# Block 0's loads in two queues, masks apart, first weights asked for ahead of the values

## The chip, the core and the metric

The kernel runs on one core of a Trainium2 chip. A core has TensorE (PE in the profile) for matrix products, VectorE (DVE), ScalarE (ACT) and GpSimd (POOL) for the rest, and SyncE (SP), which here does nothing but issue DMAs. Every engine works through its own instructions in order and waits on semaphores. SP and ACT can each issue DMAs into a hardware queue of their own; the packets of both queues run on the same 16 DMA engines. The metric is the device time of one execution in microseconds; runs are compared by their medians.

## What is computed

Three steps, one behind the other, all in fp32: attention over 4 x 8 heads of 576 positions with 64 columns, a gated feed-forward layer behind an RMS norm, and a second gated layer.

```python
mask_local = (rel >= 0) & (rel < 32)                        # heads 0..3
mask_strided = (rel >= 0) & (pos_k % 32 == pos_q % 32)      # heads 4..7
attn = softmax(where(mask, q @ k.T / 8, -1e9)) @ v
x = attn.transpose(0, 2, 1, 3).reshape(2304, 512)
x = x / sqrt(mean(x * x) + 1e-6) * rms_g
x = (silu(x @ w_gate) * (x @ w_val)) @ w_out                # 512 -> 1536 -> 512
out = (x @ w_a) * (x @ w_b) @ w_out2                        # 512 -> 1536 -> 512
```

## The kernel before

**Blocks.** The 2304 tokens are cut into six blocks t of 384 (96 positions of each of 4 batches). A block runs through attention, then through twelve chunks fc of 128 hidden columns: `mm_in` makes the gate sums `g_ps` and the value sums `v_ps` (12 matmuls each), VectorE and ScalarE make `h` of them, `split` cuts `h` into a high and a low part `hl`, and `emit_y` adds the chunk's share to `y` with 12 more matmuls. Attention of block t+1 is woven into the chunks of block t. A last stage does the second layer for all blocks.

**Products in three passes.** `mm3` makes every fp32 product of three matmuls, high by high, high by low and low by high. So weights and activations are held in two parts each. The weights arrive raw and are converted once, while block 0 runs: `words` takes two ScalarE steps (L137, L142), one VectorE step (L145), then `parts` casts on ScalarE (L150) and subtracts on GpSimd (L151). For chunk 0 the gate and the value weights are converted in two halves of 512 columns; from chunk 1 on both go through in one step of 1024. The tile `cz` between them has two buffers for gate and value weights, so that a third L142 waits for the first L151.

**Attention of block 0** is not woven into anything: until it is done, TensorE has no chunk to work on. The local heads run on TensorE in three groups g: scores (`qk`, L296), mask and scale (`smask`, L314), row maximum (`lmax`, L323), exponentials (`lexp`, L336 and L333), division (`lnorm`, L346 to L348), transposition (`pt`, L358, with the identity matrix, and `ptc`, L368), product with the values (`pv`, L378). The strided heads need no matrix product: `sqk` multiplies on GpSimd (L248) and sums on VectorE (L251), then `ssub`, `sexp` (L264), `snorm` (L270 to L273), and `spv` multiplies by the values on GpSimd (L281) and sums on VectorE (L284). The product tile has two buffers, so the third product waits for the first sum. The results `xx` (L387 high, L389 low) are the right-hand sides of chunk 0, and `rinv` (L448, L450) is the norm that all gates of the block need.

**What sets the order.** The list `LOADS0` says in which order the loads of block 0 are written, `STEPS0` the order of its steps; behind them a scheduler orders each engine's instructions by a timeline of its own. So a moved load also moves compute instructions. Before, SP issues all loads, and the constants `cst_sb` (identity, both masks and the norm's gains, 194 KB) come in one DMA behind the strided queries `qs_t` and keys `kv_t`, whose rows are 768 bytes long. There are eight completion semaphores for the DMAs; a ninth waits until the first has landed. The raw weights follow behind all of block 0's loads: `load_units(NFC)` asks for twelve units of two 512 KB tiles, gate and value weights of chunk 0 first.

## Time and profile before

| | |
|---|---|
| median of three runs | 964.13 us (962.64 to 965.04) |
| profiled execution, its own time | 965.19 us |
| its span in the trace | 963.4 us |
| busy share of the span: PE, DVE, ACT, POOL | 97 %, 65 %, 44 %, 56 % |
| mean granted clock of TensorE | 0.986 |

The profile is of one execution, 1.8 us of which lie outside the span, and this execution took 1.06 us more than the median. Times in the trace count from the start of the span. In a timeline a row is: start, duration, engine, line, operation, what is written and read, shape, count, and in brackets how long the engine sat idle before it and what ended that wait. SPq stands for the DMAs that SP issues; their duration is that of the issue. In a table of windows each engine has its busy time and its number of instructions, then come TensorE's granted clock, the share of time in which the DMA engines were busy, and GB/s.

### The profile page before, as it was taken

To read this page: it belongs to the slowest core of one execution; us is meant where nothing else is said; L and a number is where in the kernel's file an instruction comes from. 1 tells how busy PE (TensorE), PEld (TensorE's weight loads), DVE (VectorE), ACT (ScalarE), POOL (GpSimd) and SP (SyncE) were. 2 spreads that over 40 slices of the span, in tenths; PEclk is the share of its full clock that TensorE was granted. 3 is DMA by queue.
4 is the path that set the end of the run, shared out by engine and by line. 5 is a ranking of instruction groups with operands and counts; after the bars stand their busy time and mean duration, and the time that the engine had idled before them with its cause. 6 is when DMAs were issued, how large, how long until landed. Compare 5 with 4: busy or idle time off the path is not lost.

```text
span 963.4 us, 14134 instructions
## 1 busy us (share of the span) xinstructions
PE 936.9 (97%) x5324; PEld 889.0 (92%) x5324; DVE 624.8 (65%) x913; ACT 421.7 (44%) x792; POOL 541.8 (56%) x407
## 2 busy tenths in 40 slices
PE   5998999999999999999999999999999999999998
PEld 4798999999999999999999898999999999999997
DVE  5669867548818895987566378667655655464534
ACT  5987655334433433444555455435425422122110
POOL 3568946458749687969379545654734424123211
PEclk6899999999999999999999999999999999999999
DMA  9964375426534553532788975997993973753701
GB/s 344 408 258 157 110 281 195 159 99 215 175 105 149 174 179 111 177 129 66 270 332 307 358 267 202 369 422 278 359 383 118 341 295 131 290 235 147 259 31 66
DMA packets 57507, 215.55 MB, mean 224 GB/s; under 512 B 5984, under 2 KB 14816, under 8 KB 51808
## 3 DMA queue, kind: packets, MB, share of 16 engines
q1 hardware_dynamic: 57296, 214.53, 61.0%
q8 instruction: 42, 0.69, 0.3%
q14 instruction: 25, 0.20, 0.1%
q10 hardware_dynamic: 144, 0.13, 0.0%
HBM read 172.17 MB, written 42.47 MB: 223 GB/s over the span
## 4 chain that ended last, share of the span: by engine, by line
PE 65%; DVE 7%; POOL 6%; DMA 5%; ACT 4%; issue 4%; SPq 0%; DVEq 0%; ACTq 0%; POOLq 0%
PE o L925 5%; PE o L923 5%; PE o L924 5%; POOL prod L248 4%; DMA raw<-in_w 4%; PE Y L856 4%; PE Y L855 4%; PE Y L854 4%; PE y L482 3%; PE Z L856 3%; PE Z L855 3%; PE Z L854 3%; PE y L483 3%; PE X L854 3%; PE X L856 2%
## 5 line engine op out<-in xcount | busy, mean ns | idle before, releaser
L151 POOL TENSOR_TENSOR hl<-c,hl 128x384 fp32r<-128x384 f32 x72 | 77.4, 1076 | 180.2 <-ACT hl L150 173.6
L248 POOL TENSOR_TENSOR prod<-kv_t,qs_t 128x512 f32<-128x512 f32 (+12 forms) x57 | 107.3, 1903 | 21.5 <-DMA wo<-wod 9.7
L482 PE MATMUL y<-hl,wo 128*128 128x384 f32 x288 | 98.3, 345 | 4.8 <-DVE hl L507 3.7
L281 POOL TENSOR_TENSOR prod<-kv_t,S_t 128x512 f32<-128x512 f32 (+12 forms) x57 | 86.8, 1536 | 22.5 <-issue 8.2
L481 PE MATMUL v_ps<-xx,gv 128*128 128x384 f32 x288 | 97.2, 337 | 1.9 <-DVE sg L760 1.9
L481 PE MATMUL g_ps<-xx,gv 128*128 128x384 f32 x288 | 97.6, 339 | 0.6 <-DVE sg L764 0.6
L482 PE MATMUL v_ps<-xx,gv 128*128 128x384 f32 x288 | 97.6, 339 | 0.0
L483 PE MATMUL v_ps<-xx,gv 128*128 128x384 f32 x288 | 97.2, 338 | 0.0
L483 PE MATMUL g_ps<-xx,gv 128*128 128x384 f32 x288 | 97.1, 337 | 0.0
L482 PE MATMUL g_ps<-xx,gv 128*128 128x384 f32 x288 | 96.8, 337 | 0.0
L861 DVE TENSOR_TENSOR c<-c,Y 128x384 f32<-128x384 f32 x108 | 58.9, 550 | 58.0 <-PE Y L856 53.6
L483 PE MATMUL y<-hl,wo 128*128 128x384 f32 x288 | 95.4, 340 | 0.0
L507 POOL TENSOR_TENSOR hl<-h,hl 128x384 fp32r<-128x384 f32 x60 | 64.9, 1081 | 51.1 <-ACT hl L506 51.0
L284 DVE TENSOR_REDUCE xs_t<-prod 128x64 f32<-128x448 f32 (+17 forms) x57 | 85.9, 1521 | 10.5 <-POOL prod L281 9.4
L481 PE MATMUL y<-hl,wo 128*128 128x384 f32 x288 | 83.7, 342 | 3.7 <-ACT hl L506 2.1
L924 PE MATMUL o<-slab,hl 128*128 128x512 f32 x214 | 83.7, 392 | 0.0
L923 PE MATMUL o<-slab,hl 128*128 128x512 f32 x214 | 83.7, 392 | 0.0
L925 PE MATMUL o<-slab,hl 128*128 128x512 f32 x214 | 82.5, 394 | 0.0
L150 ACT CAST hl<-c 128x384 fp32r<-128x384 f32 x72 | 37.0, 514 | 94.9 <-DVE c L891 94.6
L856 PE MATMUL Y<-slab,form 128*128 128x384 f32 x216 | 73.1, 338 | 0.0
L855 PE MATMUL Y<-slab,form 128*128 128x384 f32 x216 | 73.0, 338 | 0.0
L854 PE MATMUL Y<-slab,form 128*128 128x384 f32 x216 | 73.0, 338 | 0.0
(148 smaller groups left out, 2463.5 us busy)
## 6 DMA issues: line engine op xcount, KB each, us to landing
form<-formd SPq DMA_DIRECT2D x32, 1792.0 KB, 10.6
wo<-wod SPq DMA_DIRECT2D x60, 512.0 KB, 4.1
raw<-in_w SPq DMA_DIRECT2D x40, 512.0 KB, 7.2
gv_raw<-in_w SPq DMA_DIRECT2D x32, 512.0 KB, 10.1
formd<-form SPq DMA_DIRECT2D x6, 1792.0 KB, 7.5
formd<-forms SPq DMA_DIRECT2D x6, 1792.0 KB, 12.5
slab<-x2d SPq DMA_DIRECT2D x24, 384.0 KB, 4.0
wod<-wo SPq DMA_DIRECT2D x12, 512.0 KB, 3.2
```

The costliest lines, as they stand in the source:

```text
L248: nc.gpsimd.tensor_tensor(pr, st["ks", g][:, :, :n, :], st["qs"][:, heads(g), mm:mm + 1, :].to_broadcast([128, G, n, D]), op=ALU.mult)
L281: st["pvm"] = nc.gpsimd.tensor_tensor(pr, st["vs", g][:, :, :n, :], st["S"][:, heads(g), mm, :n, None].to_broadcast([128, G, n, D]), op=AL ...
L284: st["pvr"] = nc.vector.tensor_reduce(st["xs"][:, mm, heads(g), :], pr.rearrange("p g n d -> p g d n"), axis=X, op=ALU.add)
L481: nc.tensor.matmul(out_ps, w_hi, x_hi, start=start, stop=False)
L482: nc.tensor.matmul(out_ps, w_hi, x_lo, start=False, stop=False)
L483: nc.tensor.matmul(out_ps, w_lo, x_hi, start=False, stop=stop)
L854: nc.tensor.matmul(bank(n), hi, x[p][:, 0, c], start=begins and c == 0, stop=False, skip_group_check=not begins)
L855: nc.tensor.matmul(bank(n), hi, x[p][:, 1, c], start=False, stop=False, skip_group_check=not begins)
L856: nc.tensor.matmul(bank(n), lo, x[p][:, 0, c], start=False, stop=c == 1, skip_group_check=not begins)
L923: nc.tensor.matmul(o, h[:, 0, cols], w[0], start=n == 0, stop=False)
L924: nc.tensor.matmul(o, h[:, 0, cols], w[1], start=False, stop=False)
L925: nc.tensor.matmul(o, h[:, 1, cols], w[0], start=False, stop=n == len(chunks) - 1)
```

## The change

The loads of block 0 are spread over two queues. SP keeps the local queries, the strided queries, the values and the weights; ACT issues the local keys `k_t`, the masks, the strided keys, the last third of the second half's queries, and the identity matrix. The constants are two tensors now: `mask_sb` (both masks and the gains, 130 KB) is asked for behind the first queries and keys, `cst_sb` is the identity matrix alone (64 KB) and comes later. The strided queries of every block, and the strided keys and values of block 0, are laid out on the host so that each partition reads one piece of 3072 bytes instead of four of 768. The first unit of raw weights is asked for ahead of the values. And the load of the square root's table waits for the strided exponential too.

```diff
-LOADS0 = "la0 lq ls0 cst la1 lb0 lvl1 lb1 lvl0 lv0"
+LOADS0 = "la0 masks lq ls0 la1 lb0 lb1 w0 cst lvl1 lv0 lvl0"
...
+        second = nc.scalar if t == 0 else nc.sync
...
-                nc.sync.dma_start(k_t, ktl[t, hf])
+                second.dma_start(k_t, ktl[t, hf])
...
-                nc.sync.dma_start(st["q", hf][:, 512:], qtl[t, hf, :, 512:])
+                (second if hf else nc.sync).dma_start(st["q", hf][:, 512:], qtl[t, hf, :, 512:])
...
-            nc.sync.dma_start(q_t, qs[:, :, 3 * t:3 * t + 3, :])
+            nc.sync.dma_start(q_t, qs[t])
...
-                nc.sync.dma_start(k_t, src[:, heads(g), :L, :])
+                if t == 0:
+                    (second if key == "ks" else nc.sync).dma_start(k_t, {"ks": ks0, "vs": vs0}[key])
+                else:
+                    nc.sync.dma_start(k_t, src[:, heads(g), :L, :])
...
-            with tc.issue_after(st["exp"].ins):
+            with tc.issue_after(st["exp"].ins), tc.issue_after(st["sexp"].ins):
...
-    cst_sb = const1.tile([128, 388], F32, name="cst_sb")
-    ident = cst_sb[:, 0:128]
+    cst_sb = const1.tile([128, 128], F32, name="cst_sb")
+    mask_sb = const1.tile([128, 260], F32, name="mask_sb")
+    ident = cst_sb
...
-    s0["cst"] = lambda: nc.sync.dma_start(cst_sb, cst)
+    s0["masks"] = lambda: nc.scalar.dma_start(mask_sb, masks)
+    s0["cst"] = lambda: nc.scalar.dma_start(cst_sb, cst)
+    s0["w0"] = lambda: load_units(1)
...
-    load_units(NFC)
+    load_units(NFC - 1)
```

No compute instruction is added or taken away; the line numbers of the changed kernel are up to 8 higher. The scheduler moves instructions in block 0 and at the head of block 1 on every engine; behind the first quarter of TensorE's rows the orders are the same again.

**The start, SP and ACT.** Here `q_t` and `k_t` are the local heads' queries and keys, `qs_t` and `kv_t` the strided heads', `v_t` the local values, `gv_raw` the raw weights. SP before:

```order
L207 DMA q_t<-in_qtl 128x512
L208 DMA k_t<-in_ktl 128x512
L227 DMA qs_t<-in_qs 128x4x192
L236 DMA kv_t<-in_ks 128x4x192
L569 DMA cst_sb<-in_cst 128x388
L207 DMA q_t<-in_qtl 128x512
L208 DMA k_t<-in_ktl 128x512
L213 DMA q_t<-in_qtl 128x256
L219 DMA v_t<-in_vl 128x512
L213 DMA q_t<-in_qtl 128x256
L219 DMA v_t<-in_vl 128x512
L236 DMA kv_t<-in_vs 128x4x192
```

SP now:

```order
L208 DMA q_t<-in_qtl 128x512
L228 DMA qs_t<-in_qs 128x768
L208 DMA q_t<-in_qtl 128x512
L214 DMA q_t<-in_qtl 128x256
L111 DMA gv_raw<-in_w 128x1024 x2
L220 DMA v_t<-in_vl 128x512
L238 DMA kv_t<-in_vs 128x768
L220 DMA v_t<-in_vl 128x512
L111 DMA gv_raw<-in_w 128x1024 x22
```

Five loads and the constants left SP, and two tiles of weights stand ahead of the values. ACT now, where the table load and eight exponentials in a row stood first:

```order
L209 DMA k_t<-in_ktl 128x512
L574 DMA mask_sb<-in_masks 128x260
L238 DMA kv_t<-in_ks 128x768
L209 DMA k_t<-in_ktl 128x512
L214 DMA q_t<-in_qtl 128x256
L575 DMA cst_sb<-in_cst 128x128
L340 ACT_TABLE_LOAD
L340 ACTIVATE s_t,lsm<-s_t,lmx 128x96 x4
L137 ACTIVATE gv_raw<-gv_raw 128x512
L142 ACTIVATE cz<-gv_raw 128x512
L340 ACTIVATE s_t,lsm<-s_t,lmx 128x96 x4
```

Six issues stand ahead of the table load, and the first two steps on weights stand between the exponentials of group 0 and those of group 1; before they came behind both. On VectorE, in the same place, the division of group 0 (L348 of the code before) now stands ahead of the maximum of group 1, and the third sum of the values' products stands behind one more weight step than before.

**ACT at chunk 1.** The rows where the weights of chunk 1 (128x1024) and the right-hand sides `xx` are made. Before:

```order
L137 ACTIVATE gv_raw<-gv_raw 128x1024
L142 ACTIVATE cz<-gv_raw 128x1024
L387 ACTIVATE xx<-att,cst_sb 128x384
L432 ACTIVATE sq<-att 128x384
L150 CAST gv<-cz 128x2x512
L387 ACTIVATE xx<-att,cst_sb 128x384
L432 ACTIVATE sq<-att 128x384
L387 ACTIVATE xx<-att,cst_sb 128x384 x2
```

Now:

```order
L137 ACTIVATE gv_raw<-gv_raw 128x1024
L142 ACTIVATE cz<-gv_raw 128x1024
L391 ACTIVATE xx<-att,mask_sb 128x384
L436 ACTIVATE sq<-att 128x384
L391 ACTIVATE xx<-att,mask_sb 128x384
L436 ACTIVATE sq<-att 128x384
L150 CAST gv<-cz 128x2x512
L391 ACTIVATE xx<-att,mask_sb 128x384 x2
```

The second right-hand side and its square moved ahead of the weights' cast.

**DVE late in block 0.** `hl` is the split that TensorE's y matmuls wait for, L776 and L778 the two steps before it, L145 the step on weights; L251, L260 and L346 to L348 belong to block 1's attention. Before:

```order
L778 SCALAR_TENSOR_TENSOR v_ps<-th,v_ps 128x384
L760 SCALAR_TENSOR_TENSOR sg<-g_ps,rinv 128x384
L346 TENSOR_SCALAR lsm<-lsm 64x8
L347 RECIPROCAL lrs<-lsm 64x8
L348 TENSOR_TENSOR s_t<-s_t,lrs 64x512
L251 TENSOR_REDUCE S_t<-prod 128x2x6
L776 TENSOR_TENSOR v_ps<-sg,v_ps 128x384
L145 SCALAR_TENSOR_TENSOR cz<-gv_raw,cz 128x1024
L260 TENSOR_REDUCE smx<-S_t 128x12
L507 TENSOR_TENSOR hl<-v_ps,hl 128x384
```

Now:

```order
L783 TENSOR_TENSOR v_ps<-sg,v_ps 128x384
L255 TENSOR_REDUCE S_t<-prod 128x2x5
L350 TENSOR_SCALAR lsm<-lsm 64x8
L351 RECIPROCAL lrs<-lsm 64x8
L145 SCALAR_TENSOR_TENSOR cz<-gv_raw,cz 128x1024
L352 TENSOR_TENSOR s_t<-s_t,lrs 64x512
L767 SCALAR_TENSOR_TENSOR sg<-g_ps,rinv 128x384
L785 SCALAR_TENSOR_TENSOR v_ps<-th,v_ps 128x384
L145 SCALAR_TENSOR_TENSOR cz<-gv_raw,cz 128x512
L255 TENSOR_REDUCE S_t<-prod 128x2x6
L783 TENSOR_TENSOR v_ps<-sg,v_ps 128x384
L511 TENSOR_TENSOR hl<-v_ps,hl 128x384
```

The wide step on weights stood between L778 and the split; now it stands ahead of the step that answers to L778, and a narrow one is in its place.

## Rows read from the trace of the kernel before

**Rows 1.** Windows of the whole program: busy us (instructions) by engine, PEclk, DMA share, GB/s.

```profile
10.00:34.00 24.00, 17.30 (x115) 13.69 (x115) 15.40 (x33) 19.44 (x44) 11.85 (x8) 0.59 1.03 407
...
42.00:58.00 16.00, 12.83 (x59) 11.70 (x60) 8.61 (x15) 15.97 (x24) 6.69 (x3) 0.89 1.04 406
58.00:88.00 30.00, 30.00 (x191) 29.27 (x189) 25.75 (x40) 24.27 (x60) 26.67 (x15) 1.00 0.46 153
88.00:96.00 8.00, 4.50 (x19) 4.44 (x19) 7.47 (x11) 4.60 (x9) 4.06 (x3) 0.79 0.50 172
96.00:130.00 34.00, 34.00 (x219) 32.58 (x218) 27.12 (x36) 23.30 (x40) 25.74 (x17) 1.00 0.39 140
130.00:960.00 830.00, 824.89 (x4661) 786.34 (x4659) 531.69 (x768) 324.88 (x609) 459.12 (x353) 1.00 0.60 220
```

**Rows 2.** Waits of PE from 34 us on: us in total, times, longest.

```profile
PE y L482 <- DVE hl L507: 3.7, 2, 3.5
```

**Rows 3.** Timeline of the first 25 us, the steps of block 0's attention.

```profile
0.73 1.28 ACT L336 ACT_TABLE_LOAD   x1 [0.73 <-PEq L1034]
...
5.29 1.23 PE L296 MATMUL att<-k_t,q_t 128*128 128x96 f32 x8
...
8.25 0.56 DVE L314 SCALAR_TENSOR_TENSOR s_t<-att,cst_sb 128x384 f32<-128x384 f32 x1 [7.17 <-DMA cst_sb<-in_cst]
...
9.05 0.54 DVE L323 TENSOR_REDUCE lmx<-s_t 128x4 f32<-128x384 f32 x1
...
9.63 0.38 ACT L336 ACTIVATE s_t<-s_t,lmx 128x96 f32<-128x96 f32 x1 [7.62 <-DVE lmx L323]
...
10.34 3.89 PE L296 MATMUL att<-k_t,q_t 128*128 128x96 f32 x24 [3.82 <-DMA k_t<-in_ktl]
...
12.36 0.56 DVE L314 SCALAR_TENSOR_TENSOR s_t<-att,cst_sb 128x384 f32<-128x384 f32 x1 [2.05 <-PE att L296]
...
13.54 0.37 ACT L336 ACTIVATE s_t<-s_t,lmx 128x96 f32<-128x96 f32 x1 [2.37 <-DVE lmx L323]
...
14.99 0.64 ACT L137 ACTIVATE gv_raw<-gv_raw 128x512 f32<-128x512 f32 x1
...
15.54 0.66 ACT L142 ACTIVATE cz<-gv_raw 128x512 uint32<-128x512 uint16 x1
...
24.64 1.15 ACT L137 ACTIVATE gv_raw<-gv_raw 128x1024 f32<-128x1024 f32 x1
```

**Rows 4.** The local keys' tile: issue of its DMAs in ns and us, time to landing.

```profile
L208 SPq DMA_DIRECT2D k_t<-in_ktl x2: 415/424/432, 1.2 to 4.1; - x2
...
DMA to landing us min/median/max: 2.9/4.5/6.1
```

**Rows 5.** The same of the raw gate and value weights up to 30 us.

```profile
L111 SPq DMA_DIRECT2D gv_raw<-in_w x20: 327/328/581, 8.2 to 28.6; - x20
...
DMA to landing us min/median/max: 6.2/10.2/10.8
```

**Rows 6.** Windows of 1 us while the strided queries and keys are loaded.

```profile
3.00:4.00 1.00, 1.00 (x6) 0.70 (x5) 0.00 (x0) 0.00 (x0) 0.00 (x0) 1.00 0.75 228
...
5.00:6.00 1.00, 1.00 (x8) 0.94 (x7) 0.00 (x0) 0.00 (x0) 0.00 (x0) 1.00 1.02 288
```

**Rows 7.** Timeline around chunk 1's first weights, POOL and ACT.

```profile
22.01 2.46 POOL L281 TENSOR_TENSOR prod<-kv_t,S_t 128x768 f32<-128x768 f32 x1 [1.02 <-DVE xs_t L284]
...
25.75 1.14 ACT L142 ACTIVATE cz<-gv_raw 128x1024 uint32<-128x1024 uint16 x1
...
29.29 1.04 ACT L150 CAST gv<-cz 128x1024 fp32r<-128x1024 f32 x1 [1.42 <-DVE cz L145]
...
32.02 1.17 ACT L137 ACTIVATE gv_raw<-gv_raw 128x1024 f32<-128x1024 f32 x1
```

**Rows 8.** Timeline of DVE before PE's long wait in block 0.

```profile
87.83 3.08 DVE L145 SCALAR_TENSOR_TENSOR cz<-gv_raw,cz 128x1024 uint32<-128x1024 uint32 x1
```

**Rows 9.** The window behind that wait.

```profile
91.10:94.40 3.30, 2.83 (x9) 2.84 (x10) 3.30 (x7) 2.21 (x6) 0.64 (x1) 0.50 0.72 218
```

More of the change, by code (lines that the diff above doesn't have):

```diff
@@ L77, in fused_kernel @@
 @with_exitstack
-def fused_kernel(ctx: ExitStack, tc: tile.TileContext, qtl, ktl, vl, qs, ks, vs, cst, w1, w2, out):
+def fused_kernel(ctx: ExitStack, tc: tile.TileContext, qtl, ktl, vl, qs, ks, vs, ks0, vs0, masks, cst, w1, w2, out):
     nc = tc.nc
@@ L515, in fused_kernel @@
     const1 = cpool.enter_context(tc.tile_pool(name="const1", bufs=1))
-    cst_sb = const1.tile([128, 388], F32, name="cst_sb")
-    ident = cst_sb[:, 0:128]
-    mask_a = cst_sb[:, 128:320].rearrange("p (a k) -> p a k", a=2)
-    mask_b = cst_sb[:64, 320:384].rearrange("p (a k) -> p a k", a=1)
-    g_sb = cst_sb[:, 384:388]
+    cst_sb = const1.tile([128, 128], F32, name="cst_sb")
+    mask_sb = const1.tile([128, 260], F32, name="mask_sb")
+    ident = cst_sb
+    mask_a = mask_sb[:, 0:192].rearrange("p (a k) -> p a k", a=2)
+    mask_b = mask_sb[:64, 192:256].rearrange("p (a k) -> p a k", a=1)
+    g_sb = mask_sb[:, 256:260]
     pts = [const1.tile([128, 4, 2, PB], F32, name=f"pt{hf}") for hf in range(2)]
@@ L1003, in st @@
         return a[:, 4:].reshape(B, 4, NM, W, D)
-    r["qs"] = c(st(q).transpose(0, 3, 1, 2, 4).reshape(128, 4, NM, D))
+    r["qs"] = c(st(q).transpose(0, 3, 1, 2, 4).reshape(128, 4, NB, NM // NB, D).transpose(2, 0, 1, 3, 4))
     r["ks"] = c(st(k).transpose(0, 3, 1, 2, 4).reshape(128, 4, NM, D))
     r["vs"] = c(st(v).transpose(0, 3, 1, 2, 4).reshape(128, 4, NM, D))
+    r["ks0"], r["vs0"] = (c(r[n][:, :, :NM // NB]) for n in ("ks", "vs"))
     def ok(rows, n):
@@ L1010, in ok @@
         return (j > i) & (j <= i + W), j
-    cst = np.zeros((128, 388), np.float32)
-    cst[:, 0:128] = np.eye(128)
+    cst = np.zeros((128, 260), np.float32)
     m, j = ok(128, 96)
-    cst[:, 128:224] = np.where(m & (j >= W), BIG, NEG)
-    cst[:, 224:320] = np.where(m, BIG, NEG)
-    cst[:64, 320:384] = np.where(ok(64, 64)[0], BIG, NEG)
-    cst[:, 384:] = np.asarray(inputs["moe_rms_g"]).reshape(NCC, 128).T
-    r["cst"] = cst
+    cst[:, 0:96] = np.where(m & (j >= W), BIG, NEG)
+    cst[:, 96:192] = np.where(m, BIG, NEG)
+    cst[:64, 192:256] = np.where(ok(64, 64)[0], BIG, NEG)
+    cst[:, 256:] = np.asarray(inputs["moe_rms_g"]).reshape(NCC, 128).T
+    r["masks"] = cst
+    r["cst"] = np.eye(128, dtype=np.float32)
     def weights(a, b, o):
```

## The prediction, made before the changed kernel ran

> **What bounds the kernel now.** I read the table of windows first, because shares over the whole span say nothing about a change in the first 30 us. From 130 to 960 us TensorE is busy 824.89 of 830 us, from 58 to 88 and from 96 to 130 us without a gap [rows 1]. So the program is one long TensorE stretch, and a load at the start can only shorten what comes ahead of it. From 10 to 34 us TensorE does little that counts, and the DMA engines are busy throughout (share 1.03, 407 GB/s). From 42 to 58 us the bound is ScalarE, 15.97 of 16 us busy, while TensorE has 12.83 [rows 1]: block 0's weights are converted there. From 88 to 96 us TensorE has 4.50 of 8 us; its wait for VectorE's split of 3.5 us lies there [rows 2]. Behind 58 us the DMA share is 0.52 or less until 130 [rows 1], so loads have slack.
>
> Then the timeline of the start. VectorE's first mask step stands at 8.25 us, 7.17 us idle, ended by the DMA of the constants; the scores it wants were done at 5.29 + 1.23 = 6.52. The second scores start at 10.34 because the second keys land then: issued at 4.1, 6.1 to landing [rows 3, 4]. In both waits ScalarE stands idle, 7.62 and 2.37 us [rows 3]. ScalarE is the engine with the long row of work from there on, so what fills or removes its idle time moves everything behind it.
>
> **Step 1, the masks.** They land early now and the scores decide: mask step at 6.6, its maximum next (the change's order has no sum in between), 0.56 + 0.54, first exponential at 7.7 instead of 9.63: 1.9 us earlier. If the masks came as late as 8.2 this would be nothing. The price is on ScalarE: six issues of about 0.42 us (SP's issue of the same keys [rows 4]), the last two waiting for the keys' and the masks' landing, and then the table load of 1.28 us, which was done by 2.0 [rows 3]. The first two loads of before needed 2.9 us from issue (the shorter of the two landings) [rows 4], so I put keys and masks at 3.7 to 5.0, the table at 6.5: hidden under the wait for the scores and the maximum until 7.7, with 1.2 us to spare. Were that cover gone, each us of delay would cost one.
>
> **Step 2, the second scores.** Up to the second keys 1,986 KB stood in the queue; now 1,922 KB in two queues count (896 on SP, 1,026 on ACT). At the old pace they land at 9.9 instead of 10.2. A faster pace is possible: while the strided rows of 768 bytes pass, the engines are busy (1.02) and move only 288 GB/s, against 407 later, and in 3 to 4 us a quarter of their time is free [rows 6, 1]. 768 KB at 407 instead of 288 save 0.8 us, the free time perhaps 0.5: 8.6 at the earliest. I take 9.2, the middle. The scores need 2.0 us as before (10.34 to 12.36), the mask step is at 11.2, and the second exponential follows after the 1.18 us of before plus the division of group 0, which the new order puts ahead of the maximum (a step like the maximum's, 0.54), less the small step that left (0.1): 12.8 instead of 13.54, 0.7 earlier (0 to 1.4).
>
> Here the Trainium skill speaks against the change, on the page "DMA: Bandwidth & Descriptors": under "Issuing engines are not separate DMA queues" it says that DMAs issued from several engines run on the same 16 DMA engines, so that a second issuer saves the issue time alone, and under "Specifications" that rows of 512 bytes or more run at line rate. By the two this step would be worth 0. The second rule does not fit [rows 6], the first may; it is a rival below.
>
> **Step 3, chunk 0's weights.** A pair of weight steps takes 1.2 us (0.64 and 0.66, overlapping). The first pair moves from behind the second exponentials (14.99) into ScalarE's gap before them, from 9.3 to 12.8; for this its tile must land by 11.6. Before, it landed at 8.2 + 6.2 = 14.4 at the earliest [rows 5]; now 2,754 KB of loads count up to it instead of 3,650, which at the 407 GB/s of the queue is 2.3 us less: 12.1. I expect it between 10.5 (faster pace of step 2) and 12.1; either way it fits in part. Between 14.99 and 24.64, the start of chunk 1's weights [rows 3], ScalarE loses that 1.2 us and a wait of about 0.6 us for the transposed rows. So chunk 1's first step could start at 24.64 - 0.7 - 1.8 = 22.1.
>
> **Step 4, what is late next.** It is GpSimd. Chunk 1's second step (25.75) needs a buffer that GpSimd frees when it has split chunk 0's first half, and that comes behind the third product of the values, at 22.01 after a wait of 1.02 us for VectorE's first sum [rows 7]. In the new order that sum stands behind one more weight step; this step needs ScalarE's third pair, which ends about 3.0 us ahead of chunk 1's start, at 19.1. With 0.7 for the weight step and 0.36 for the sum, the product starts at 20.3, 1.7 earlier. So of the 2.5 us of step 3, 1.7 get through here: chunk 1's second step at 24.05.
>
> **Step 5, a gap that closes.** ScalarE waited 1.42 us ahead of chunk 1's cast (29.29) for VectorE [rows 7]. The new order puts the second right-hand side and its square in that wait, 0.95 us. Chunk 2's weights, at 32.02 before, start at 32.02 - 1.7 - 0.95 = 29.4: 2.6 earlier. The norm, the first gates and TensorE's first chunk hang on the same row and move with it.
>
> **The sum.** 42 to 58 us is ScalarE's stretch without idle time, then come GpSimd, VectorE and TensorE in turn; no row there is tied to a time of the DMA queue. So the 2.6 us pass through: 965.19 - 2.6 = 962.6 for the profiled execution, which took 1.06 more than the median, hence 961.5 against the median of 964.13. Bounds from the steps: 1.6 (step 2 at 0, a third of the gap left) to 3.3 (step 2 at 1.4): 960.8 to 962.5. Other blocks' strided queries in one piece: I count 0, TensorE waits for none of them; at most some 0.1 us each of queue time.
>
> What the sum cannot give is the new order of block 0. Differences of orders have no row, so I bound them by the one wait that is there: 3.5 us [rows 2], behind a weight step of 3.08 us on VectorE [rows 8], and then 3.3 us in which TensorE, after that wait, was granted 0.50, the lower of its two levels, 1.2 GHz [rows 9]; a stretch at half pace gives back 1.65. Together 5.1 us either way.
>
> **Rivals.** (a) *The long wait shrinks.* The split now follows three short steps behind the one it depends on, not the wide weight step. If 1.1 to 3.5 us of it go: 958.0 to 960.4. Against it: the wide step moved ahead of that earlier step, so the chain may be as long. (b) *A new wait eats the gain.* That same place: the step that answers to L778 waits behind a weight step of 1.2 to 3.08 us, TensorE waits for it: 962.7 to 964.6, with half of the following slow stretch up to 966. (c) *The loads do not come earlier*, the first rule above as a mechanism: both queues at the old pace, keys at 9.9, weights at 12.1. Step 2 gives 0, step 3 loses half of its pair, step 4 gives 0.9 and step 5 stays: 1.8 in all, 962.3; if the gap of step 5 does not close, 963.2. (d) *Slower*: a second long wait with a slow stretch behind it, 5.1 us, against a gain at its lower end of 1.6: 967.6. It decides once TensorE, between 58 and 88 us, meets a wait long enough that the granted clock falls; GpSimd and VectorE are busy 26.67 and 25.75 of 30 us there [rows 1], so the room is small.
>
> **How the numbers follow.** The measurement can tell about 0.3 %, 2.9 us: below 961.2 is faster, above 967.0 slower. The sum goes through (960.4 to 962.7): 0.58, of which 0.21 lies below 961.2. (a) 0.22, faster. (b) 0.11, same. (c) 0.03, same. (d) 0.06, slower. So faster 0.43, same 0.51, slower 0.06. The likeliest time is 961.5. The range of 958.0 to 964.8 holds the sum, nearly all of (a), most of (b) and (c), and leaves out (d) and the tails, together about 0.16.
>
> **What would show it.** In the changed kernel's timeline: first mask step at 6.6 behind the scores, not behind a DMA; first exponential at 7.7; second scores at 8.6 to 9.9; a pair of 512-wide weight steps ahead of the second exponentials; third product of the values at 20.3; chunk 2's first weight step at 29.4. If these stand and the time does not follow, look at TensorE's waits and the granted clock between 58 and 130 us. The table load ending behind 7.7, or keys landing behind 10 us, would make steps 1 or 2 wrong.

## The result and the profile after

The changed kernel takes 969.29 us (median of six runs, 968.69 to 970.79), the kernel before on the same chip 962.35 (961.00 to 965.04): a ratio of 1.0071 with a 95 % interval of 1.0054 to 1.0088. It is about 7 us slower, where 961.5 was forecast. The profiled execution took 969.16 us (its span is 967.0). That is 4.0 us over the 965.19 of the profiled execution of before, which took 2.8 more than the median of these runs, so the two traces show a little over half of the difference.

First the table of windows of the changed kernel, in the stretches of [rows 1] (columns as there), with the part behind 130 us in two stretches; then the kernel before in these two:

```profile
10.00:34.00 24.00, 17.39 (x118) 13.77 (x118) 18.20 (x35) 20.36 (x40) 11.83 (x9) 0.62 1.03 409
42.00:58.00 16.00, 12.84 (x70) 12.06 (x71) 9.35 (x16) 15.97 (x25) 6.73 (x3) 1.00 1.04 411
58.00:88.00 30.00, 28.34 (x176) 26.76 (x174) 27.43 (x37) 22.53 (x57) 25.28 (x14) 1.00 0.39 133
88.00:96.00 8.00, 6.54 (x39) 5.97 (x39) 7.55 (x17) 6.62 (x11) 2.15 (x3) 1.00 0.57 200
96.00:130.00 34.00, 31.23 (x198) 29.48 (x197) 24.50 (x28) 19.59 (x35) 25.27 (x17) 1.00 0.26 93
...
130.00:210.00 80.00, 76.13 (x469) 72.54 (x469) 50.51 (x82) 38.13 (x85) 42.55 (x39) 1.00 0.60 202
210.00:960.00 750.00, 746.25 (x4178) 711.45 (x4177) 484.49 (x686) 291.84 (x530) 417.21 (x316) 1.00 0.61 223
```

Before:

```profile
130.00:210.00 80.00, 78.62 (x490) 76.18 (x489) 47.93 (x82) 33.27 (x80) 45.71 (x40) 1.00 0.57 190
210.00:960.00 750.00, 746.28 (x4173) 710.15 (x4171) 483.76 (x687) 291.62 (x529) 413.41 (x314) 1.00 0.61 223
```

Behind 210 us the two kernels are alike (746.25 and 746.28 of 750). The loss lies ahead of it: from 58 to 88 and from 96 to 130 us TensorE was busy without a gap [rows 1], and now lacks 1.7 and 2.8 us; from 130 to 210 it lacks 3.9 where it lacked 1.4. The granted clock is 1.00 in all these stretches: the half pace of [rows 9] is gone, and the kernel is slower all the same.

From 40 to 130 us, TensorE's waits of 0.25 us and more were four before: the long one of [rows 2] and three of 0.95 to 1.35 us. Now there are nine. The waits of the changed kernel from 34 us on (us in total, times, longest):

```profile
PE y L485 <- ACT wo L150: 3.6, 4, 1.6
PE g_ps L485 <- DVE sg L767: 2.9, 3, 1.6
PE v_ps L485 <- DVE sg L767: 2.7, 2, 1.8
PE y L485 <- ACT hl L510: 2.5, 2, 2.0
...
PE y L486 <- POOL hl L511: 1.3, 3, 0.7
PE att L362 <- DVE s_t L352: 1.1, 1, 1.1
```

None is longer than 2.0 us, and the wait that led in [rows 2] is gone. The start, as the steps of the prediction named it, in the timeline of the changed kernel (answers to [rows 3, 7]):

```profile
6.48 0.56 DVE L318 SCALAR_TENSOR_TENSOR s_t<-att,mask_sb 128x384 f32<-128x384 f32 x1 [5.39 <-DMA mask_sb<-in_masks]
6.76 1.28 ACT L340 ACT_TABLE_LOAD   x1 [6.76 <-DMA mask_sb<-in_masks]
8.05 0.38 ACT L340 ACTIVATE s_t<-s_t,lmx 128x96 f32<-128x96 f32 x1
8.73 4.12 PE L300 MATMUL att<-k_t,q_t 128*64 128x64 f32 x24 [2.55 <-DMA q_t<-in_qtl]
10.63 0.67 ACT L137 ACTIVATE gv_raw<-gv_raw 128x512 f32<-128x512 f32 x1 [1.03 <-DMA gv_raw<-in_w]
12.80 0.38 ACT L340 ACTIVATE s_t<-s_t,lmx 128x96 f32<-128x96 f32 x1 [0.94 <-DVE lmx L327]
...
21.94 1.48 POOL L285 TENSOR_TENSOR prod<-kv_t,S_t 128x768 f32<-128x768 f32 x1 [1.55 <-DVE xs_t L288]
23.49 1.15 ACT L137 ACTIVATE gv_raw<-gv_raw 128x1024 f32<-128x1024 f32 x1
...
30.13 1.16 ACT L137 ACTIVATE gv_raw<-gv_raw 128x1024 f32<-128x1024 f32 x1
...
37.51 0.58 ACT L452 ACTIVATE rms_t<-att,eps_sb 128x384 f32<-128x384 f32 x1 [1.87 <-PE att L440]
```

So the loads do what they were expected to do: weights of chunk 1 1.2 us and of chunk 2 1.9 us earlier than before. A ruler for the rest is the start of the norm's reciprocal on VectorE, `rinv`, once a block. It stands at 38.53, 128.99 and 210.75 us before, at 38.12, 130.20 and 214.71 after: 0.4 us ahead, then 1.2 behind, then 4.0 behind. From the first to the second is called block 0's stretch below, to the third block 1's.

### The profile page after: what moved, and what is told of

It is laid out like the page before. It is cut to its first block, busy times and chain, and to the rows that moved or that the text cites. A ratio compares the mean times of both kernels' runs of the same rounds, so it can differ in the third digit from the quotient of the medians.

```text
span 967.0 us, 14132 instructions
## 1 busy us (share of the span) xinstructions
PE 935.3 (97%) x5324; PEld 885.5 (92%) x5324; DVE 631.6 (65%) x913; ACT 424.0 (44%) x794; POOL 538.1 (56%) x407
## 4 chain that ended last, share of the span: by engine, by line
PE 67%; DVE 10%; POOL 6%; DMA 6%; ACT 5%; issue 4%; SPq 0%; POOLq 0%; DVEq 0%; ACTq 0%
PE o L932 5%; PE o L931 5%; PE o L930 5%; DMA raw<-in_w 4%; PE Y L863 4%; PE Y L862 4%; PE Y L861 4%; POOL prod L252 3%; PE Z L863 3%; PE Z L862 3%; PE Z L861 3%; PE y L486 3%; PE g_ps L487 3%; PE X L861 3%; PE g_ps L485 2%
## 5 line engine op out<-in xcount | busy, mean ns | idle before, releaser
L285 POOL TENSOR_TENSOR prod<-kv_t,S_t 128x512 f32<-128x512 f32 (+12 forms) x57 | 85.9, 1519 | 28.3 <-issue 10.5
L486 PE MATMUL y<-hl,wo 128*128 128x384 f32 x288 | 96.2, 339 | 1.4 <-POOL hl L511 1.3
L487 PE MATMUL y<-hl,wo 128*128 128x384 f32 x288 | 92.7, 335 | 0.0
L485 PE MATMUL y<-hl,wo 128*128 128x384 f32 x288 | 84.0, 344 | 7.7 <-ACT wo L150 3.6
## 6 DMA issues: line engine op xcount, KB each, us to landing
form<-formd SPq DMA_DIRECT2D x32, 1792.0 KB, 10.5
```

What stands on the lines that cost most here:

```text
L285: st["pvm"] = nc.gpsimd.tensor_tensor(pr, st["vs", g][:, :, :n, :], st["S"][:, heads(g), mm, :n, None].to_broadcast([128, G, n, D]), op=AL ...
L485: nc.tensor.matmul(out_ps, w_hi, x_hi, start=start, stop=False)
L486: nc.tensor.matmul(out_ps, w_hi, x_lo, start=False, stop=False)
L487: nc.tensor.matmul(out_ps, w_lo, x_hi, start=False, stop=stop)
```

## Experiments

**Loads or order.** The edit moves loads and, through the scheduler, compute instructions. To part them, each engine's compute instructions were pinned to a written order (each number is an instruction's place in the program) by edges between neighbours:

```diff
+        keep_order(tc)
...
+def keep_order(tc):
+    ins = list(tc.nc.cur_bb.bb.instructions)
+    info = mybir.DependencyInfo(mybir.DependencyClass.NoSync, mybir.DependencyReason.DATA)
+    for name, runs in ORDER.items():
...
+        for k, j in zip(want, want[1:]):
+            tc.add_manual_dep(own[j], own[k].name, info, reason="order")
```

Four kernels use it: e1 is the changed kernel with the order of before, e2 the kernel before with the new order. e3 is the changed kernel with the new order only up to chunk 0's first gates, the old one behind; e4 the kernel before with its own order up to there and the new one behind. VectorE's numbers show where they part (- is the new order, + that of before; a+n stands for n instructions from a on): e1 has both pieces with +, e2 both with -, e3 the first with - and the second with +, e4 the other way round.

```diff
-0+3 6+2 3 13 4 14 8 15 9 5 10+2
+0+3 6 3 7 4 8 13 9 5 14 10+2
...
-58 73 88 77 70 45 74 46 75 101 93 64 94
+58 73 88 77 70 74+3 45+2 101 79 93+2 87
```

> The changed kernel's loads (two queues, masks apart, rows in one piece, first weights ahead of the values), but PE, DVE, ACT and POOL issue their instructions in the order of the kernel before, written out as edges between neighbours. Theory L (the order from 45 us on is what costs): the new waits of TensorE on the casts of wo (3.6 us in the changed kernel) and on the gate step L767 (2.9 and 2.7 us) are gone, and part of the earlier start comes through: 960.0 to 962.5, ratio to before 0.9975 to 1.000. Rival D (the loads themselves cost, whatever the order, because block 0 starts earlier and meets the same later waits with the clock or the DMA engines against it): 966 to 969, ratio over 1.004.

> The kernel before with all its old loads, but with the changed kernel's order of instructions on PE, DVE, ACT and POOL. Theory L: as slow as the changed kernel or slower, since an order made for early loads also waits for late ones: 968.5 to 972, ratio 1.006 to 1.010. Rival D: the order alone costs nothing, 962 to 964, ratio 1.000 to 1.002.

> The changed kernel's loads, the changed kernel's order up to the first gate steps of chunk 0 (PE's first 200 instructions, DVE's first 50, ACT's first 45), and the order of the kernel before behind that, where the two hold the same instructions. Theory L: the start's gain without the late waits; of the 1.9 us by which chunk 2's weights start earlier, about 0.4 was left at the first rms step (37.51 against 37.92), so 959.5 to 962.0, ratio 0.997 to 1.000, about as e1 and perhaps 0.5 better. Rival D: 966 to 969. Rival S (the new order of the start, the ones products split in two on PE, is what costs): over 964, and e1 clearly faster.

> The kernel before in loads and in its order up to the first gate steps of chunk 0, and behind that the changed kernel's order alone. Theory L: the whole loss of 7 us is here: 967.5 to 970.5, ratio 1.005 to 1.0085. Rival D and rival S: 962 to 964, ratio 1.000 to 1.002.

Measured (median us, ratio to the kernel before on the same chip with its interval): e1 960.72, 0.9976 [0.9965, 0.9988]; e2 973.62, 1.0107 [1.0090, 1.0124]; e3 961.12, 0.9980 [0.9971, 0.9988]; e4 970.58, 1.0077 [1.0063, 1.0090]. The loads alone gain 2.4 us, the order alone costs 10.5, and 0.9976 times 1.0107 is 1.0083, within the interval of the changed kernel. The order at the start does no harm once the loads are early (e3 beside e1), and costs 3.0 us when they are late (e2 beside e4); the order behind chunk 0's first gates costs 7.5 us with the old loads (e4). The norms say where: 37.25, 126.38 and 206.30 us in e3, 38.12, 130.20 and 214.71 in the changed kernel, which has the same loads and start. Block 0's stretch is 3.0 us longer (92.08 against 89.13), block 1's 4.6 (84.51 against 79.92). The waits of TensorE of 0.25 us and more, added up from the two timelines, make 10.6 us against 7.6 from 40 to 130 us, and 3.7 against none from 130 to 210: the 3.0 of block 0 and most of the 4.6 of block 1.

**Is it the weight steps that VectorE holds?** In the changed kernel TensorE waits 1.56 us at 89.46 for the output weights `wo`. Its timeline on VectorE, GpSimd and ScalarE there:

```profile
85.86 2.89 DVE L145 SCALAR_TENSOR_TENSOR cz<-gv_raw,cz 128x512 uint32<-128x512 uint32 x1
...
85.56 2.64 POOL L151 TENSOR_TENSOR gv<-cz,gv 128x1024 fp32r<-128x1024 f32 x1 [2.24 <-ACT gv L150]
...
88.79 0.62 ACT L150 CAST wo<-cz 128x512 fp32r<-128x512 f32 x1 [2.33 <-DVE cz L145]
```

The narrow weight step, 0.65 to 0.69 us where nothing runs on GpSimd, takes 2.89: it ends 0.55 us behind GpSimd's instruction (85.56 + 2.64 = 88.20, 88.75). The wide step of [rows 8] ended at 90.91 in the same way, 1.08 behind GpSimd. The time so lost between 40 and 135 us, summed over VectorE's steps with two inputs, is about 9.5 us before and in e1, 13.8 after and in e4 (an estimate: the length of each step less that of its kind alone). That looked like the cause. m1 is e4, m2 the kernel before, both with one input less in the step, which leaves the low bits of the weights out of the result:

```diff
-            nc.vector.scalar_tensor_tensor(z(), raw[:, :, 1], 3, z(), op0=ALU.logical_shift_left, op1=ALU.bitwise_or)
+            nc.vector.tensor_scalar(z(), raw[:, :, 1], 3, None, op0=ALU.logical_shift_left)
```

> e4 (old loads, old start, the changed kernel's order from chunk 0's gates on) with one edit: the VectorE step on weights (L145) reads one SBUF operand, the raw words shifted by 3, and leaves out the OR with the tile cz that ACT wrote; so the low bits of the weights are missing. Theory P (the late order costs because more of VectorE's two-operand steps meet a running GpSimd instruction and stand still until it ends: 13.8 us of them between 40 and 135 us against 9.5 before, of which L145 has 10.1): the wide step takes about 1.2 us and the narrow one 0.7 wherever GpSimd is, TensorE's waits on the wo casts (3.9 us) and on the gate step (2.9 and 2.1) fall to half or less, time 960 to 966, and at most 4 us over m2. Rival Q (the casts and gate steps just stand too far back in their engines' rows, whatever a step on VectorE costs): 6 to 8 us over m2.

> The kernel before, loads and order alike, with the same edit: L145 reads one SBUF operand and leaves out the OR with cz. Theory P: the wide step at 87.8 us takes 1.2 us instead of 3.08, TensorE's wait of 3.5 us falls to about 1.6 or less and the slow stretch behind it may go: 957 to 961. Rival Q: no change beyond 1 us, 962 to 963.5, since the wait's end would then be another's.

m1 took 967.99 us, 1.0046 [1.0029, 1.0063], m2 959.61, 0.9962 [0.9947, 0.9976]. The difference of 8.4 us is as large as without the edit. But the edit did not do what it was for. In m1's timeline the step with one input still stands still beside GpSimd:

```profile
81.16 2.19 DVE L145 TENSOR_SCALAR cz<-gv_raw 128x1024 uint32<-128x1024 uint32 x1
...
84.80 2.39 DVE L145 TENSOR_SCALAR cz<-gv_raw 128x512 uint32<-128x512 uint32 x1
```

Alone it takes 0.68 and 0.42 us. So the pair tells nothing on the hold as such. It does tell that this shorter step helps: some 3 us in either order (e4 to m1, the kernel before to m2). The stretches of m1 and m2 differ by 0.6 us in block 0 (88.58 and 87.95) and by 5.0 in block 1 (85.97 and 81.00), which turned the view to block 1. Without the edit block 0's stretch is 92.40 in e4 and 90.46 before, so in block 0 the shorter step takes back more of the new order; the traces of before and of m2 both have stretches at a lower granted clock there, so no more is read from this.

**The long wait of before.** If a held step is what TensorE waits for, steps that it waits for should pass ahead of it. e5 is e1 with four small steps ahead of the wide weight step on VectorE:

```diff
 L783 TENSOR_TENSOR v_ps<-sg,v_ps 128x384
-L145 SCALAR_TENSOR_TENSOR cz<-gv_raw,cz 128x1024
+L511 TENSOR_TENSOR hl<-v_ps,hl 128x384
+L785 SCALAR_TENSOR_TENSOR v_ps<-th,v_ps 128x384
+L767 SCALAR_TENSOR_TENSOR sg<-g_ps,rinv 128x384
 L264 TENSOR_REDUCE smx<-S_t 128x12
...
+L145 SCALAR_TENSOR_TENSOR cz<-gv_raw,cz 128x1024
```

e6 goes on from e5: around 50 us, two `tanh` (L769) and two casts of `hl` (L510) on ScalarE, and the steps of the same chunks on VectorE, stand ahead of weight steps. One piece of it on ScalarE:

```diff
-L137 ACTIVATE gv_raw<-gv_raw 128x1024
-L769 ACTIVATE th<-sg 128x384
+L769 ACTIVATE th<-sg 128x384
+L137 ACTIVATE gv_raw<-gv_raw 128x1024
 L510 CAST hl<-v_ps 128x384
```

e7 moves chunk 0's first gate step (L767) ahead of a weight step too, and chunk 2's gate step ahead of a value step (not shown):

```diff
-L145 SCALAR_TENSOR_TENSOR cz<-gv_raw,cz 128x1024
-L767 SCALAR_TENSOR_TENSOR sg<-g_ps,rinv 128x384
-L145 SCALAR_TENSOR_TENSOR cz<-gv_raw,cz 128x1024
+L767 SCALAR_TENSOR_TENSOR sg<-g_ps,rinv 128x384
+L145 SCALAR_TENSOR_TENSOR cz<-gv_raw,cz 128x1024 x2
```

> e1 (the changed kernel's loads, the old order) with one move on VectorE: at 87 us the split hl (L511), the value step (L785), the next gate step (L767) and the small row maximum stand ahead of the wide weight step instead of behind it. Theory P: the wide step cannot start before GpSimd's split ends anyway, so it ends when it ended before, and TensorE's wait of 3.5 us is nearly gone, with the stretch at the lower clock behind it perhaps: 955.5 to 958, ratio 0.992 to 0.995. Rival W (the wait comes back a chunk later on the wo cast or on GpSimd's split): 959 to 961.

> e5 with a second move, on ACT and VectorE between 44 and 56 us: the tanh of chunks 1 and 2 and the casts hl of chunks 0 and 1 stand ahead of weight steps that nobody waits for yet, where ACT is busy without a gap and TensorE waited 1.4 us for the cast hl. If that wait alone goes: 1 to 1.5 us below e5. If the slow stretch behind it (51 to 57 us) goes too: up to 3 us below e5. Rival: ACT's stretch is the bound and TensorE waits later for weights instead, same as e5 or slower.

> e6 with two more moves on VectorE: the first gate step (sg of chunk 0) ahead of a weight step, and the gate step of chunk 2 ahead of the value step that waits for chunk 1's tanh. TensorE waited 1.19 and 1.89 us for these two in e6 (at 41.2 and 47.6 us). If ACT's stretch without a gap until 58 us is the bound, nothing: 959.5 to 960.5; if TensorE's waits count there, 958 to 959.5.

e5: 960.83 us, 0.9974 [0.9959, 0.9988]; e6: 959.98, 0.9963 [0.9948, 0.9978]; e7: 960.29, 0.9966 [0.9951, 0.9981]. In e1's timeline the wait on TensorE, VectorE's wide step and GpSimd's instruction beside it, then the same in e5's:

```profile
90.44 0.69 PE L507 MATMUL y<-hl,wo 128*128 128x384 f32 x1 [3.48 <-DVE hl L532]
...
86.71 3.07 DVE L166 SCALAR_TENSOR_TENSOR cz<-gv_raw,cz 128x1024 uint32<-128x1024 uint32 x1
...
84.88 3.83 POOL L172 TENSOR_TENSOR gv<-cz,gv 128x1024 fp32r<-128x1024 f32 x1
```

```profile
87.37 0.44 PE L486 MATMUL y<-hl,wo 128*128 128x384 f32 x1 [0.33 <-DVE hl L511]
...
88.30 1.81 DVE L145 SCALAR_TENSOR_TENSOR cz<-gv_raw,cz 128x1024 uint32<-128x1024 uint32 x2
...
84.93 2.85 POOL L151 TENSOR_TENSOR gv<-cz,gv 128x1024 fp32r<-128x1024 f32 x1
```

The wait of 3.5 us is gone, and VectorE gained as well: starting 1.6 us later, when GpSimd is done, the wide step and the narrow one behind it take 1.81 together. Yet e5 is no faster than e1. One thing that the record shows is that the 3.5 us are not a fixed length: e1's profiled execution, at 962.98 us, is above e1's median. The same place in e1_again, the same program, profiled at 960.42 us (below):

```profile
86.62 0.44 PE L486 MATMUL y<-hl,wo 128*128 128x384 f32 x1 [1.75 <-DVE hl L511]
...
84.75 1.21 DVE L145 SCALAR_TENSOR_TENSOR cz<-gv_raw,cz 128x1024 uint32<-128x1024 uint32 x1
...
84.61 3.59 POOL L151 TENSOR_TENSOR gv<-cz,gv 128x1024 fp32r<-128x1024 f32 x1
```

Here the wide step began almost together with GpSimd's instruction, took 1.21 us, and TensorE waited 1.75. Behind it, e5's waits (0.72 us at 107, 0.83 at 118, 0.88 at 130.5) have their like in e1_again (0.41 at 106, 0.79 at 117, 0.88 at 129). So rival (a) priced by its full length a wait that another execution has at half of it. Why taking 1.4 us out of it gains nothing is not shown: e5's own profiled execution has a stretch at a lower granted clock (0.72 from 51 to 57 us), so its later times cannot be set against e1_again's. e6 has the lowest median of the kernels that compute the whole result, 2 to 5 us under the kernel before by its interval; what it has over e1 is not resolved, and e7 is not faster than e6.

**Which block's order costs.** f1 has the changed kernel's loads and its order through block 0 and block 1's first gates, the old order behind; f2 has the old order through block 0 and the new one in block 1 alone. On VectorE (- is f1, + is f2; from 150 on f1 has the old order and f2 the new one):

```diff
-0+3 6+2 3 13 4 14 8 15 9 5 10+2
+0+3 6 3 7 4 8 13 9 5 14 10+2
...
-142 145 147 143 146 144 148 150 149 151 156 159 157 152+4
+136 142 147 143 150 144 151+5 149 159 156+3 160+2
```

f3 is the changed kernel with four exponentials of block 1 moved ahead of a Silu on ScalarE, which saves two of 40 table loads:

```diff
-L772 ACT_TABLE_LOAD
-L772 ACTIVATE sg<-sg 128x384
-L340 ACT_TABLE_LOAD
 L340 ACTIVATE s_t,lsm<-s_t,lmx 128x96 x4
+L772 ACT_TABLE_LOAD
+L772 ACTIVATE sg<-sg 128x384
```

> The changed kernel's loads and the changed kernel's order through block 0 and the first gates of block 1 (PE's first 603 instructions), the old order behind that. Between the profiles of the changed kernel and of e3 the stretch from the first norm (rinv) to the second is 92.08 against 89.13 us, and the first norm stands 0.9 later. Theory T (each block's own order costs what its own stretch shows): 961.1 + 0.9 + 2.9 = 965, range 963.5 to 966. Rival U (all of the loss is block 0's, block 1 only inherits a bad start): 968 to 970.

> The changed kernel's loads, the old order through block 0 and the first gates of block 1, and the changed kernel's order in block 1 alone. The stretch from the second norm to the third is 84.51 us in the changed kernel and 79.92 in e3, with two more table loads on ACT there (40 in the program against 38). Theory T: 960.9 + 4.6 = 965.5, less what stands at the block's border, range 963 to 966.5. Rival U: 960 to 962.

> The changed kernel, loads and order, with one move on ACT in block 1: the four exponentials of the second local group (168.9 us), whose maximum is there since 158.2, stand ahead of the Silu at 167.05, next to the eight exponentials before it, so that two table loads of 1.28 us go. Theory E (these loads delay the cast hl and the division that TensorE waits for at 171 and 173 us, 0.5 and 1.1 us, and what follows at 178.6 and 180.7, 0.6): 966.5 to 968, 1.3 to 2.8 us below the changed kernel's 969.3. Rival (TensorE waits for the Silu instead, which comes 1.3 us later): 969 to 970.

f1: 971.31 us, 1.0082 [1.0067, 1.0097]; f2: 962.91, 1.0000 [0.9989, 1.0012]; f3: 967.57, 1.0047 [1.0032, 1.0063]. The theory that each block's order costs its own half (T: 965 for f1) fell. Block 0's order alone costs all of it, 10 us over e3, and more than half of that shows in block 1, whose order is the old one: its stretch is 87.08 us in f1 against 79.92 in e3. f2's 2 us over e1 lie at the edge of the intervals, and e1_again's interval (below) overlaps f2's. f3's interval overlaps that of the changed kernel (1.0054 to 1.0088), and its profiled block 1 is no shorter (85.30 against 84.51): inconclusive.

How the end of block 0 reaches into block 1 is seen where block 2's strided queries and keys are loaded, for the products that GpSimd makes during block 1. The rows of f1 on SP, GpSimd, VectorE and TensorE:

```profile
134.95 0.32 SPq L794 DMA_DIRECT2D wod<-wo  x1
...
135.38 0.66 SPq L228 DMA_DIRECT2D qs_t<-in_qs  x1
...
142.62 2.35 POOL L252 TENSOR_TENSOR prod<-kv_t,qs_t 128x448 f32<-128x448 f32 x2 [10.98 <-DMA wo<-wod]
...
143.78 0.62 DVE L255 TENSOR_REDUCE S_t<-prod 128x7 f32<-128x448 f32 x1 [6.30 <-POOL prod L252]
...
144.92 0.44 PE L485 MATMUL v_ps<-xx,gv 128*128 128x384 f32 x1 [2.08 <-DVE sg L771]
...
146.94 1.94 PE L300 MATMUL att<-k_t,q_t 128*128 128x96 f32 x8 [1.41 <-DMA v_t<-in_vl]
```

and of e3:

```profile
125.20 0.32 SPq L815 DMA_DIRECT2D wod<-wo  x1
...
125.70 0.33 SPq L249 DMA_DIRECT2D qs_t<-in_qs  x1
...
132.01 2.42 POOL L273 TENSOR_TENSOR prod<-kv_t,qs_t 128x448 f32<-128x448 f32 x2 [8.76 <-DMA kv_t<-in_ks]
```

SP issues the store of the last converted output weights, `wod`, and right behind it block 2's first load. In e3 that load goes out at 125.70, in f1 at 135.38, in the changed kernel at 135.78. GpSimd's first product comes 5.5 to 7.2 us later and begins a chain: VectorE waits for the product, the gate step `sg` stands behind VectorE's sum, and TensorE waits for `sg`. (The row of f1 names another DMA, `wo`, as the last to land; it was issued at 137.21, right behind block 2's queries and first keys.) The new order converts the last output weights late on ScalarE: the changed kernel's last two casts of `wo` start at 130.07 and 133.83, behind the table loads of the norm and of `tanh`; e3's last is done by 124.5.

**That reach by itself.** h1 is e1 with this moved: the conversion of the last output weights (chunk 11, second half) goes behind the norm of block 1, two steps on ScalarE and two on VectorE. Besides, a memset of 0.24 us on VectorE comes later and one `hl` step goes ahead of its neighbour. On ScalarE:

```diff
-L142 ACTIVATE cz<-raw 128x512
-L150 CAST wo<-cz 128x512
 L452 ACT_TABLE_LOAD
 L452 ACTIVATE rms_t<-att,eps_sb 128x384
 L769 ACT_TABLE_LOAD
 L769 ACTIVATE th<-sg 128x384
+L142 ACTIVATE cz<-raw 128x512
+L150 CAST wo<-cz 128x512
```

e1_again is e1 once more on h1's chip.

> e1 (the changed kernel's loads, the old order) with one thing of the new order added: the last weights of block 0, the output weights of chunk 11, are converted behind block 1's norm instead of ahead of it (ACT: cz and the cast wo behind rms_t and a tanh; VectorE: its two steps behind the reciprocal). Theory V (the next attention's tiles take the place of the conversion's tiles, and SP issues in order, so block 2's strided queries and keys are asked for only when the last conversion is done: 135.4 in f1 against 125.7 in e3, and GpSimd's products start 10.6 us later): here the loads go out at about 131 to 132 and the stretch from the second norm to the third grows by 2 to 6 us: 963 to 966.5. Rival U2 (the late loads are hidden; the 7 us that f1 loses in block 1 come from elsewhere in block 0's order): 960.5 to 962.

> e1 once more, on the same chip as its variants here: 960.2 to 961.5 by its first result of 960.72; it is what h1 and l2 are compared with.

h1: 964.09 us, 1.0013 [0.9997, 1.0029]; e1_again: 961.69, 0.9983 [0.9967, 1.0000]. Four steps that each take under 0.7 us cost 2.4 us by the medians, though the intervals of the ratios overlap slightly. At a like granted clock the two part: the executions with a mean clock of 0.989 or more took 962.5 to 964.1 us in h1 and 960.0 to 961.3 in e1_again. The traces show where: the store goes out at 129.66 instead of 124.75, GpSimd's first product starts at 135.47 instead of 131.62, behind a wait of 12.47 us for the keys (8.83 in e1_again), VectorE waits 4.46 us for it, and block 1's stretch is 85.22 instead of 80.50 us, against a gain of 1.4 us ahead of the norm. The windows from 130 to 210 us of h1, then of e1_again:

```profile
130.00:210.00 80.00, 76.65 (x474) 73.40 (x473) 46.24 (x81) 31.80 (x80) 46.70 (x41) 1.00 0.56 189
```

```profile
130.00:210.00 80.00, 80.00 (x504) 78.07 (x503) 49.52 (x82) 33.05 (x79) 49.12 (x43) 1.00 0.56 184
```

TensorE has 3.4 us without work, as in the changed kernel (3.9 us), and none without that move. So the late conversion is shown as a cause of block 1's loss: 4.7 us of stretch for a store that is 4.9 us late. That it makes all of f1's 7.2 us, where the store is 9.8 us late, is argued from the same rows. Two things hold block 2's loads back there, SP's order of issue and, by the program, the room of their tiles, which the conversion's tiles occupy until they are done; which of the two holds longer was not tried.

**What in the loads gains.** l1 is e1 with every load issued by SP; l2 is e1 with the rows of 768 bytes of before:

```diff
-        second = nc.scalar if t == 0 else nc.sync
+        second = nc.sync
...
-    s0["masks"] = lambda: nc.scalar.dma_start(mask_sb, masks)
-    s0["cst"] = lambda: nc.scalar.dma_start(cst_sb, cst)
+    s0["masks"] = lambda: nc.sync.dma_start(mask_sb, masks)
+    s0["cst"] = lambda: nc.sync.dma_start(cst_sb, cst)
```

```diff
-            nc.sync.dma_start(q_t, qs[t])
+            nc.sync.dma_start(q_t, qs[:, :, 3 * t:3 * t + 3, :])
...
-                    (second if key == "ks" else nc.sync).dma_start(k_t, {"ks": ks0, "vs": vs0}[key])
+                    (second if key == "ks" else nc.sync).dma_start(k_t, src[:, heads(g), :L, :])
```

> e1 (the changed kernel's loads, the old order of instructions) with all loads issued from SP in the changed kernel's sequence, ACT issuing none: masks still apart, rows still in one piece, first weights still ahead of the values. Theory N (the second queue is worth nothing, or less: its issues on ACT hold the table load until 6.8 us): 959.5 to 961.5, within 0.5 us of e1's 960.7 or below it. Rival M (the second queue is what brings the keys and masks early, since SP would need about 0.45 us for each issue and waits for a free semaphore at the ninth): 961.5 to 963, first mask step behind 7 us.

> e1 with the strided queries, keys and values laid out as before, four rows of 768 bytes for each partition instead of one piece of 3072; two queues, masks apart and the weights ahead stay. If the rows cost what windows of before showed (288 GB/s against 407 with the engines busy), the second keys land 0.5 to 0.9 us later than in e1 (9.04) and the time grows by as much: 961 to 962. Rival: only the sequence of loads matters, no difference to e1 in the landing.

l1: 961.41 us, 0.9986 [0.9974, 0.9999]; l2: 961.72, 0.9989 [0.9974, 1.0003]; both within the interval of e1_again, so in time neither edit is resolved. The traces part them. Windows of l1 while the first loads pass, then of e1_again, then of l2:

```profile
4.00:5.00 1.00, 1.00 (x7) 0.74 (x5) 0.00 (x0) 0.00 (x0) 0.00 (x0) 1.00 0.98 285
...
6.00:7.00 1.00, 1.00 (x6) 0.91 (x5) 0.00 (x0) 0.00 (x0) 0.00 (x0) 1.00 1.05 280
```

```profile
4.00:5.00 1.00, 1.00 (x7) 0.73 (x5) 0.00 (x0) 0.00 (x0) 0.00 (x0) 1.00 1.05 409
...
6.00:7.00 1.00, 0.34 (x4) 0.17 (x2) 0.56 (x1) 0.29 (x1) 0.00 (x0) 1.00 1.05 417
```

```profile
4.00:5.00 1.00, 1.00 (x7) 0.74 (x5) 0.00 (x0) 0.00 (x0) 0.00 (x0) 1.00 1.08 370
```

In these windows the DMA engines are as busy with one queue and move 280 to 285 GB/s, long rows or not (288 in [rows 6], with short ones); with two queues they move 409 to 417, or 370 with the short rows of l2. Over all of 2 to 9 us it is 2.04 MB in l1 against 2.40 in e1_again, added up from the same view. The second scores start at 10.34 us before [rows 3], 10.41 in l1, 9.19 in l2 and 9.08 in e1_again: the second queue brings 1.3 us, the long rows 0.1. My expectation for l2, 0.5 to 0.9 us, fell. Chunk 1's weights (24.71 in l1, 23.69 in l2, 23.49 in e1_again) say the same.

## Why the prediction was wrong

**Steps 1 and 2** came out near their numbers. The mask step stands at 6.48 us (6.6 foretold), the first exponential at 8.05 (7.7), the second at 12.80 (12.8). Two signs of step 1 failed by a little. The mask step's row names the masks' DMA and not the scores, which were done at 6.18. And the table load ended behind 7.7, at 8.04, and cost 0.35 us; its row names the same DMA as what held ScalarE until 6.76. The second scores start at 9.14 (9.2 foretold): the row at 8.73 begins with two matmuls of the third group, 64 columns wide, and the first with 96 columns follows at 9.14. Of step 2, the reason was half wrong: the slow pace of [rows 6] went away with the second queue, and the rows of 768 bytes cost only 0.1 us (l2). The Trainium skill, "DMA: Bandwidth & Descriptors", section "Issuing engines are not separate DMA queues", lets a second issuer save issue time alone. The second keys are in fact issued 1.4 us earlier (2.13 us, in l1 3.54), which by itself would fit the 1.3 us of their landing; but the pace rose too, from 280 to 417 GB/s at the same busy share, and there the runs decide against its letter. Rival (c), whose keys kept the old pace until 9.9 us, did not happen.

**Step 3** came out at 23.49 instead of 22.1; **step 4** failed. The third product starts at 21.94, 0.07 us earlier than before instead of 1.7. GpSimd waits for VectorE's sum, and this stands behind two weight steps that together took 2.13 us (at 19.41), beside a product on GpSimd. I had put 0.7 for one of them, the time of a step with nothing beside it. Chunk 1's second step still came at 24.69 (24.05 foretold), since the product itself took 1.48 us instead of the 2.46 of [rows 7], and **step 5** closed most of its gap (0.56 us left of 1.42), so that chunk 2's weights stand at 30.13, 1.9 us earlier instead of 2.6.

**The gain of the loads passed through to the end, but only with the old order.** The changed kernel's first norm is only 0.4 us earlier, since ScalarE waits 1.87 us for TensorE's product with the ones (37.51), which the new order puts among gate matmuls. With the order of before, the norm stands 1.2 us earlier in e1 and 1.6 in e1_again, and the loads gain 2.4 us by the medians in e1 (1.2 to 3.4 by its interval) and 1.0 in e1_again (0 to 3.2); 2.6 was forecast, with bounds of 1.6 to 3.3. That term had the right sign and about the right size, perhaps too large.

**The step that failed is the price of the new order.** I bounded it by one long wait with its slow stretch, 5.1 us "either way", looked for it between 58 and 130 us, and gave rival (d) a chance of 0.06. It cost 7.5 us (e4) to 10 us (f1 over e3). Three things were wrong in it. First, GpSimd at 26.67 and VectorE at 25.75 of 30 us were taken for safety ("the room is small"); but TensorE had no gap there, so that each step that came late could only cost, and from 58 to 88 us it lost 1.7 us. Second, the loss came in waits of 0.3 to 2.0 us for three other engines, with the clock at 1.00 throughout, and a bound drawn from the one long wait does not hold a sum of short ones: nine of them make 10.6 us from 40 to 130 us. Third, more than half of it lies behind 130 us, in a block whose own order costs about 2 us by the medians (f2), because late output weights hold back the next block's loads (h1). Rival (d) had the sign, not the mechanism: its place was a second long wait and a granted clock that falls, and neither is in the trace. Rival (a)'s long wait did vanish, and e5, where it is 0.33 us, is no faster than e1 by the medians.

What stays open: which of the moved steps in block 0 make its 3.0 us. The waits are there, for weight casts and gate steps behind held weight steps, and e6 and the shorter step of m1 and m2 gain where these are relieved, but no run takes the hold away and leaves the rest. That the hold is the cause of block 0's loss is argued, not shown.

## What to carry to other kernels

Where a scheduler sets the order, an edit of the loads is two edits; pin the order of before on the new loads and look at both, since here the loads gained 1 to 2 us and the order that came with them lost 7.5 to 10. Before a wait in one profile is priced, see whether a second execution has it at the same length. A stretch in which the bounding engine has no gap is the one to fear for when orders change, and a bound for it has to count many short waits. And when buffers are handed from one block's work to the next block's loads, look past the stretch that was edited: what ends late in one block starts late in the next.
